# Reading the turned left-over rows back from DRAM: two plain DMAs of 64 rows ahead of the 128, in place of one with a repeated dimension

## The chip, the cores and the metric

The kernel runs on one core of one Trainium2 chip. The metric is the device time of one execution in microseconds (us). The time before is 1430.58 us, the median of 3 runs (1426.18 to 1431.6).

## The reference

Two parts follow one another. The first is a causal convolution over 7 taps whose weights are a softmax per token and head. The second is a gated feed-forward layer on the result. `x` is 4 x 4096 x 192, so there are 16384 tokens of 192 channels, in 8 heads of 24; the feed-forward width is 1536. All is float32.

```python
w = softmax(weight_gen, axis=-1)              # [B, S, 8 heads, 7 taps]
x_pad = concat([zeros(B, 6, 192), x], axis=1)
out = einsum('bshk,bskhg->bshg', w, windows_of_7(x_pad))
...
g = out @ w_gate                              # 192 -> 1536
y = (g * sigmoid(g)) * (out @ w_val) @ w_out  # 1536 -> 192
```

## The kernel before

The 16384 tokens lie as 128 partitions of 128 tokens. A block `g` takes 4 tokens (JG) of every partition, 512 tokens in all, and there are 32 blocks. For the matmuls a block is needed turned, channels on the partitions: 192 channels are one half of 128 and a left-over half of 64. Each float32 operand is split into a `hi` part in the fp32r format and the rest `lo`, and the products of the parts are summed in PSUM.

The feed-forward part goes in steps, 12 to a block (one for each 128 of the 1536 hidden channels), 384 in all. In a step TensorE makes the gate and the value sums (`up`, lines 500, 503 and 512). ScalarE takes the `silu` of one (`sg`, L520), VectorE multiplies (`h`, L534), ScalarE rounds it (`hi`, L535) and VectorE takes the rest (`lo`, L537). Two and three steps later TensorE multiplies by `w_out` (`dn`, L564, L573). There are four PSUM banks for `up`, two to a step; `sg` and `h` are what frees them.

The convolution of block `g` runs on VectorE beside the steps of block `g - 1`: products with a tap (`mul`, L234) and sums (`add`, L262), spread over the steps by hand (the function `spread` and the table `todo`). From block 2 on the result is turned in three moves (`turn_ops`). VectorE transposes within tiles of 32 x 32 (`blocks`, L341, into `cut`). Four DMAs on SP's queue write the tiles to a DRAM buffer `turned`, where they land in turned order (L352). Then SP reads them back into the tile `t32` of [128, 2, 512] (`places`): `t32[:, 0]` gets the 128 rows (L357). `t32[:, 1]` gets the 64 left-over rows twice, in partitions 0 to 63 and again in 64 to 127 (L358), since the left-over matmuls of the gate sums use the lower partitions and those of the value sums the upper ones. Reads wait until all four writes have landed.

Three steps after `blocks` and `places` comes the split of the turned block (`split_ops`), in the order `high(1)`, `low(1)` in one step and `high(0)`, `low(0)` in the next: ScalarE makes `xhi` (L378) and VectorE `xlo` (L385), the left-over half first. Engines work strictly in order, so what stands behind a waiting `xhi` on ScalarE, and behind a waiting `xlo` on VectorE, waits too. In the step of `high(1)` VectorE also has the first two products of the next block behind `xlo`.

This sets the order (`s0` is four steps before block `g - 1` begins):

```python
moves, halves = turn_ops(g)
at = s0 + NF - 3
spread(moves, at, at + 1)
spread(halves, at + 3, at + 5)
```

Of the kernel before, what the change touches and what calls it, by code (L numbers as in the profile page):

```python
# [18 lines left out]
def dynconv_glu_kernel(  # L19
# [23 lines left out]
    nc = tc.nc  # L43
    B, S, D = x.shape
# [3 lines left out]
    P = 128  # L48
    T = B * S // P
    PAD = K - 1  # L50
    DB = D - P
    JG = 4
    NC = JG * P
# [223 lines left out]
    LOW, HIGH = slice(0, DB), slice(DB, P)  # L277
# [54 lines left out]
    def turn_ops(g):  # L332

        whole = {}

        def blocks():
            cut = att.tile([P, JG, D], F32, tag="aside", name="cut", bufs=ASIDE)
            cut = whole["cut"] = cut.rearrange("p t d -> p (t d)").rearrange(
                "p (i t c) -> p i t c", i=NB, t=JG
            )  # L340
            nc.vector.transpose(  # L341
                cut, xatt[g][:, :, 0:D].rearrange("p t (i r) -> p i t r", i=NB)
            )

        def places():
            t32 = att.tile([P, JG, 2 * P], F32, tag="xatt", name="t32")
            t32 = whole["t32"] = t32.rearrange("p t d -> p (t d)").rearrange(
                "p (i n) -> p i n", i=2
            )
            there = away.tile([NB, Q, P // Q, P], F32, tag="turned", name="turned")  # L350
            for j in range(P // Q):
                nc.sync.dma_start(  # L352
                    out=there[:, :, j].rearrange("i r n -> r i n"),
                    in_=whole["cut"][j * Q : (j + 1) * Q].rearrange("r i t c -> r i (t c)"),
                )
            rows = there.rearrange("i r j n -> (i r) (j n)")
            nc.sync.dma_start(out=t32[:, 0], in_=rows[0:P])  # L357
            nc.sync.dma_start(  # L358
                out=t32[:, 1], in_=rows[P:D].unsqueeze(0).to_broadcast([2, DB, NC])
            )  # L360

        def part(n):
            def go():
                if n == 0:
                    t32 = whole["t32"]
                    whole["split"] = split_ops(g, (t32[:, 0], t32[:, 1]))
                whole["split"][n]()

            return go

        return [blocks, places], [part(n) for n in range(4)]

    def split_ops(g, ps):
        hi = [xts.tile([P, NC], F32R, tag=f"xhi{half}", name="xhi") for half in range(2)]

        def high(half):
            def go():
                nc.scalar.activation(out=hi[half], in_=ps[half], func=AF.Copy)  # L378

            return go  # L380

        def low(half):
            def go():
                lo = xts.tile([P, NC], F32R, tag=f"xlo{half}", name="xlo")
                nc.vector.tensor_tensor(  # L385
                    out=lo, in0=ps[half], in1=hi[half].bitcast(F32), op=ALU.subtract
                )
                xT[g, half] = hi[half], lo

            return go  # L390

        return [high(0), low(0), high(1), low(1)] if g < MOVED else [high(1), low(1), high(0), low(0)]
# [383 lines left out]
```

## Time and profile before

| | us |
|---|---|
| median of 3 runs | 1430.58 |
| the profiled execution | 1429.34 |
| its span, first to last instruction | 1427.6 |
| TensorE matmul busy (PE) | 1322.0 (93%) |
| VectorE busy (DVE) | 1026.0 (72%) |
| ScalarE busy (ACT) | 594.7 (42%) |
| GpSimd busy (POOL) | 62.4 (4%) |
| mean granted TensorE clock | 0.968 |

The profile is of one execution. Busy time of an engine is the time in which an instruction of it ran; matmuls are pipelined and their ends are modelled, so a busy TensorE isn't one at its peak. The list of waits gives the idle time of an engine just before an instruction and puts it down to what ended last. The windows give for a stretch of the span the busy time of each engine, the granted clock (1.00 is the level of 2.4 GHz, 0.50 that of 1.2) and the mean busy share of the 16 DMA engines.

### The profile page before, as it was taken

To read this page: it belongs to the slowest core of one execution; us is meant where nothing else is said; L and a number is where in the kernel's file an instruction comes from. 1 tells how busy PE (TensorE), PEld (TensorE's weight loads), DVE (VectorE), ACT (ScalarE), POOL (GpSimd) and SP (SyncE) were. 2 spreads that over 40 slices of the span, in tenths; PEclk is the share of its full clock that TensorE was granted. 3 is DMA by queue.
4 is the path that set the end of the run, shared out by engine and by line. 5 is a ranking of instruction groups with operands and counts; after the bars stand their busy time and mean duration, and the time that the engine had idled before them with its cause. 6 is when DMAs were issued, how large, how long until landed. Compare 5 with 4: busy or idle time off the path is not lost.

```text
span 1427.6 us, 31213 instructions
## 1 busy us (share of the span) xinstructions
PE 1322.0 (93%) x13184; PEld 1243.8 (87%) x13184; DVE 1026.0 (72%) x1413; ACT 594.7 (42%) x1049; POOL 62.4 (4%) x62
## 2 busy tenths in 40 slices
PE   5888999999999989999999999999999999999997
PEld 5677999888998978988898988988988898989997
DVE  6987677676777756787776687766677776677753
ACT  5444344433344434444443443433353433444443
POOL 4840000000000000000000000000000000000000
PEclk9799999999999999999999999999999999999999
DMA  6501211212211121211212111221211212110110
GB/s 173 172 12 46 77 36 26 65 27 77 58 44 49 35 65 38 72 34 41 77 27 77 38 33 56 54 66 38 74 26 27 68 35 77 38 27 24 38 38 12
DMA packets 63249, 74.88 MB, mean 52 GB/s; under 512 B 6024, under 2 KB 52616, under 8 KB 61316
## 3 DMA queue, kind: packets, MB, share of 16 engines
q1 hardware_dynamic: 63108, 72.88, 19.4%
q8 instruction: 103, 1.69, 0.5%
q14 instruction: 38, 0.31, 0.1%
HBM read 48.48 MB, written 24.38 MB: 51 GB/s over the span
## 4 chain that ended last, share of the span: by engine, by line
PE 47%; DMA 22%; DVE 19%; ACT 5%; SPq 4%; issue 2%; ACTq 0%; DVEq 0%
DMA t<-turned 17%; PE up L500 12%; PE up L512 11%; PE dn L564 10%; PE up L503 10%; DVE h L534 4%; DMA turned<-cut 4%; DVE prod L234 3%; SPq L352 3%; PE dn L573 3%; DVE xatt L234 2%; DVE cut L341 2%; ACT sg L520 2%; DVE xlo L385 2%; DVE lo L537 1%
## 5 line engine op out<-in xcount | busy, mean ns | idle before, releaser
L564 PE MATMUL dn<-wo,hi 64*128 64x384 f32 x2976 | 612.2, 351 | 1.4 <-ACT osb L589 1.1
L573 PE MATMUL dn<-wo,lo 64*128 64x192 f32 x2976 | 541.4, 252 | 0.3 <-DVE lo L537 0.3
L564 PEld LDWEIGHTS dn<-wo,hi 64*128 64x128 f32 x2976 | 507.0, 189 | 15.7 <-ACT osb L589 3.2
L573 PEld LDWEIGHTS dn<-wo,lo 64*128 64x128 f32 x2976 | 474.4, 191 | 3.5 <-DVE lo L537 0.5
L535 ACT ACTIVATE hi<-h 128x512 fp32r<-128x512 f32 x372 | 235.4, 633 | 386.2 <-DVE h L534 385.6
L534 DVE TENSOR_TENSOR h<-up,sg 128x512 f32<-128x512 f32 x372 | 256.1, 689 | 191.6 <-ACT sg L520 191.4
L520 ACT ACTIVATE sg<-up 128x512 f32<-128x512 f32 x384 | 228.0, 594 | 304.4 <-PE up L512 283.4
L500 PE MATMUL up<-xhi,wb_hi 64*128 64x512 f32 x768 | 250.0, 428 | 75.5 <-DVE h L534 55.5
L537 DVE TENSOR_TENSOR lo<-h,hi 128x512 fp32r<-128x512 f32 x372 | 254.9, 685 | 83.1 <-ACT hi L535 83.1
L512 PE MATMUL up<-xhi,wa_hi 64*128 64x512 f32 x768 | 233.0, 424 | 8.3 <-POOLq L282 8.2
L500 PE MATMUL up<-xlo,wb_hi 64*128 64x512 f32 x768 | 230.9, 404 | 1.5 <-DVE xlo L385 1.5
L500 PE MATMUL up<-xhi,wb_lo 64*128 64x512 f32 x768 | 227.3, 401 | 0.0
L503 PE MATMUL up<-xhi,wa_lo 64*128 64x512 f32 x768 | 227.1, 400 | 0.0
L503 PE MATMUL up<-xhi,wa_hi 64*128 64x512 f32 x768 | 226.5, 399 | 0.2 <-ACT xhi L378 0.2
L503 PE MATMUL up<-xlo,wa_hi 64*128 64x512 f32 x768 | 225.6, 397 | 0.0
L500 PEld LDWEIGHTS up<-xhi,wb_hi 64*128 64x128 f32 x768 | 136.6, 186 | 98.0 <-DVE h L534 70.0
L512 PE MATMUL up<-xhi,wa_lo 64*128 64x512 f32 x768 | 220.8, 395 | 0.0
L512 PE MATMUL up<-xlo,wa_hi 64*128 64x512 f32 x768 | 220.4, 393 | 0.0
L262 DVE TENSOR_TENSOR xatt<-xatt,prod 128x768 f32<-128x768 f32 x183 | 176.0, 962 | 0.0
L234 DVE TENSOR_TENSOR prod<-xt,wt 128x768 f32<-128x768 f32 x183 | 175.4, 958 | 0.2
L512 PEld LDWEIGHTS up<-xhi,wa_hi 64*128 64x128 f32 x768 | 137.0, 189 | 11.2 <-POOLq L282 11.2
L503 PEld LDWEIGHTS up<-xlo,wa_hi 64*128 64x128 f32 x768 | 139.1, 190 | 7.7 <-DVE xlo L385 0.5
(60 smaller groups left out, 1365.6 us busy)
## 6 DMA issues: line engine op xcount, KB each, us to landing
xt<-in_x_dram SPq DMA_DIRECT2D x14, 1344.0 KB, 11.6
t<-turned SPq DMA_DIRECT2D x60, 256.0 KB, 2.7
turned<-cut SPq DMA_DIRECT2D x120, 96.0 KB, 2.1
out_dram<-osb SPq DMA_DIRECT2D x116, 96.0 KB, 1.9
raw<-in_moe_w_out_dram SPq DMA_DIRECT2D x12, 192.0 KB, 2.8
wt<-in_weight_gen_dram SPq DMA_DIRECT2D x3, 672.0 KB, 9.6
raw<-in_moe_w_gate_dram SPq DMA_DIRECT2D x12, 128.0 KB, 2.1
raw<-in_moe_w_val_dram SPq DMA_DIRECT2D x12, 128.0 KB, 3.0
```

Of the source, the lines that this page charges most:

```text
L234: engine.tensor_tensor(out=into.rearrange("p t (h i) -> p t h i", h=H), in0=src, in1=w, op=ALU.mult)
L262: nc.vector.tensor_tensor(out=a, in0=a, in1=tmp.pop(k), op=ALU.add)
L352: nc.sync.dma_start(out=there[:, :, j].rearrange("i r n -> r i n"), in_=whole["cut"][j * Q : (j + 1) * Q].rearrange("r i t c -> r i (t c)"),)
L500: nc.tensor.matmul(ps, w[r, fs], m[r], start=(n == 0), stop=False)
L503: ins = nc.tensor.matmul(sums[i], w[r, i, fs], m[r], start=False, stop=False)
L512: ins = nc.tensor.matmul(sums[i], w[r, i, fs], m[r], start=False, stop=(n == len(full) - 1))
L520: nc.scalar.activation(out=sg, in_=sums[0], func=AF.Silu)
L534: nc.vector.tensor_tensor(out=h, in0=sums[1], in1=sg, op=ALU.mult)
L535: nc.scalar.activation(out=hi, in_=h, func=AF.Copy)
L537: nc.vector.tensor_tensor(out=lo, in0=h, in1=hi.bitcast(F32), op=ALU.subtract)
L564: nc.tensor.matmul(acc[t], hi[r, cs], wo[r, f].rearrange("p a d -> p (a d)"), start=opens, stop=False,)
L573: nc.tensor.matmul(acc[t][:, 0:D], lo[r, cs], wo[r, f, 0], start=False, stop=closes)
```

## The change

In `places` the read of the left-over rows with a repeated dimension goes. In its place two plain DMAs read the same 64 rows, one into partitions 0 to 63 (`LOW`) and one into 64 to 127 (`HIGH`) of `t32[:, 1]`. Both are issued ahead of the read of the 128 other rows, which came first before. Lines behind it move up by one, so L520 becomes L519 and so on.

```diff
             rows = there.rearrange("i r j n -> (i r) (j n)")
+            for r in (LOW, HIGH):
+                nc.sync.dma_start(out=t32[r, 1], in_=rows[P:D])
             nc.sync.dma_start(out=t32[:, 0], in_=rows[0:P])
-            nc.sync.dma_start(
-                out=t32[:, 1], in_=rows[P:D].unsqueeze(0).to_broadcast([2, DB, NC])
-            )
```

On SP's queue, in one of the blocks in which the load of `xt` follows, this is the order before, from the four writes to `turned` to the stores of a result (`t_16792` is the tile `t32` of that block; `DMAHW0` to `DMAHW7` are the semaphores that DMAs count in turn):

```order
L352 DMA turned<-cut 32x6x128 [waits DVE_49]
L352 DMA turned<-cut 32x6x128
L352 DMA turned<-cut 32x6x128 [waits DMAHW2_49]
L352 DMA turned<-cut 32x6x128 [waits DMAHW3_49]
L357 DMA t_16792<-turned 128x512 [waits DMAHW3_49,DMAHW2_49,DMAHW4_49,DMAHW1_49,DMAHW0_49]
L358 DMA t_16792<-turned 128x1x512 [waits DMAHW5_49]
L144 DMA xt<-in_x_dram 128x2688 [waits DMAHW6_49]
L605 DMA out_dram<-osb 32x4x192 [waits DMAHW7_49,DVE_49]
```

And this is the same place of the changed kernel:

```order
L352 DMA turned<-cut 32x6x128 [waits DVE_49]
L352 DMA turned<-cut 32x6x128 [waits DMAHW2_49]
L352 DMA turned<-cut 32x6x128 [waits DMAHW3_49]
L352 DMA turned<-cut 32x6x128 [waits DMAHW4_49]
L358 DMA t_16817<-turned 64x512 [waits DMAHW4_49,DMAHW3_49,DMAHW5_49,DMAHW2_49,DMAHW1_49]
L358 DMA t_16817<-turned 64x512 [waits DMAHW6_49]
L359 DMA t_16817<-turned 128x512 [waits DMAHW7_49]
L144 DMA xt<-in_x_dram 128x2688 [waits DMAHW0_49]
L604 DMA out_dram<-osb 32x4x192 [waits DVE_49]
```

Two reads became three, the 128 rows went from first to third, and the first read waits for the four writes as before.

On ScalarE the split of a block stands like this before, with the `silu` and the rounding of the steps around it:

```order
L520 ACTIVATE sg<-up 128x512 [waits PE_49,Activation_49]
L535 ACTIVATE hi<-h 128x512 [waits DVE_49]
L378 ACTIVATE xhi<-t_8734 128x512 [waits DMAHW3_49]
L520 ACTIVATE sg<-up 128x512 [waits PE_49,Activation_49]
L535 ACTIVATE hi<-h 128x512 [waits DVE_49]
L378 ACTIVATE xhi<-t_8734 128x512 [waits DMAHW2_49]
```

And in the changed kernel:

```order
L519 ACTIVATE sg<-up 128x512 [waits PE_49,Activation_49]
L534 ACTIVATE hi<-h 128x512 [waits DVE_49]
L377 ACTIVATE xhi<-t_8746 128x512 [waits DMAHW7_49,DMAHW6_49]
L519 ACTIVATE sg<-up 128x512 [waits PE_49,Activation_49]
L534 ACTIVATE hi<-h 128x512 [waits DVE_49]
L377 ACTIVATE xhi<-t_8746 128x512 [waits DMAHW0_49]
```

Nothing moved there; the first `xhi` waits for two reads where it waited for one.

## Rows read from the trace of the kernel before

**Rows 1.** The page, the chain that ended last, shares by line.

```profile
DMA t<-turned 17%; PE up L500 12%; PE up L512 11%; PE dn L564 10%; PE up L503 10%; DVE h L534 4%; DMA turned<-cut 4%; DVE prod L234 3%; SPq L352 3%; PE dn L573 3%; DVE xatt L234 2%; DVE cut L341 2%; ACT sg L520 2%; DVE xlo L385 2%; DVE lo L537 1%
```

**Rows 2.** Waits of the whole span: us in total, times, longest.

```profile
ACT xhi L378 <- DMA t<-turned: 107.2, 30, 7.1
```

**Rows 3.** Timeline of SP: start, length in us; one block, then the worst block.

```profile
462.37 1.80 SPq L352 DMA_DIRECT2D turned<-cut  x4
465.87 0.34 SPq L357 DMA_DIRECT2D t<-turned  x1
466.26 0.50 SPq L358 DMA_DIRECT2D t<-turned  x1
...
509.95 0.50 SPq L358 DMA_DIRECT2D t<-turned  x1
```

**Rows 4.** Timeline of ScalarE in that first block; brackets: idle before, and what ended it.

```profile
460.13 0.60 ACT L520 ACTIVATE sg<-up 128x512 f32<-128x512 f32 x1 [1.23 <-PE up L512]
...
469.77 0.60 ACT L520 ACTIVATE sg<-up 128x512 f32<-128x512 f32 x1 [1.22 <-PE up L512]
471.12 0.63 ACT L535 ACTIVATE hi<-h 128x512 fp32r<-128x512 f32 x1 [0.76 <-DVE h L534]
474.19 0.63 ACT L378 ACTIVATE xhi<-t 128x512 fp32r<-128x512 f32 x1 [2.43 <-DMA t<-turned]
```

**Rows 5.** Landings: of `t` where it could be matched; a 64-partition weight load.

```profile
DMA to landing us min/median/max: 2.6/2.7/2.8
...
raw<-in_moe_w_gate_dram SPq DMA_DIRECT2D x12, 64.0 KB, 2.4
```

**Rows 6.** Windows: stretch, length, busy us of each engine, clock, DMA share, GB/s.

```profile
470.00:473.50 3.50, 3.50 (x40) 3.48 (x38) 1.39 (x2) 1.00 (x2) 0.00 (x0) 1.00 0.13 51
```

**Rows 7.** Timelines of VectorE, then TensorE, behind that wait.

```profile
474.85 0.69 DVE L385 TENSOR_TENSOR xlo<-t,xhi 128x512 fp32r<-128x512 f32 x1 [2.37 <-ACT xhi L378]
476.33 0.95 DVE L234 TENSOR_TENSOR prod<-xt,wt 128x768 f32<-128x768 f32 x1
477.20 0.68 DVE L534 TENSOR_TENSOR h<-up,sg 128x512 f32<-128x512 f32 x1
...
477.94 0.49 PE L500 MATMUL up<-xhi,wb_hi 64*128 64x512 f32 x1 [1.50 <-DVE h L534]
```

**Rows 8.** Windows, five steps from the waiting one, per block; five of thirty, sum.

```profile
123.23:146.10 22.87, 19.20 (x172) 15.96 (x169) 17.11 (x26) 6.95 (x13) 0.00 (x0) 0.93 0.26 70
...
385.17:405.63 20.46, 18.37 (x173) 16.74 (x172) 14.96 (x21) 7.08 (x13) 0.00 (x0) 0.92 0.09 33
428.09:447.24 19.15, 17.05 (x174) 15.45 (x172) 14.44 (x21) 6.86 (x12) 0.00 (x0) 1.00 0.21 68
469.77:487.88 18.11, 16.61 (x173) 15.31 (x172) 13.72 (x20) 6.85 (x12) 0.00 (x0) 1.00 0.03 12
...
1368.18:1384.25 16.07, 16.07 (x174) 16.07 (x172) 8.02 (x12) 7.08 (x12) 0.00 (x0) 1.00 0.04 12
sum 601.73, PE 531.96 PEld 484.99 DVE 423.52 ACT 209.34 POOL 0.00; mean PE 17.73 PEld 16.17 DVE 14.12 ACT 6.98 POOL 0.00
```

**Rows 9.** Timeline of ScalarE, the waiting `xhi` of the other blocks named.

```profile
134.47 0.63 ACT L378 ACTIVATE xhi<-t 128x512 fp32r<-128x512 f32 x1 [3.62 <-DMA t<-turned]
...
390.60 0.63 ACT L378 ACTIVATE xhi<-t 128x512 fp32r<-128x512 f32 x1 [3.44 <-DMA t<-turned]
...
433.52 0.63 ACT L378 ACTIVATE xhi<-t 128x512 fp32r<-128x512 f32 x1 [3.45 <-DMA t<-turned]
...
519.48 0.63 ACT L378 ACTIVATE xhi<-t 128x512 fp32r<-128x512 f32 x1 [7.11 <-DMA t<-turned]
...
1372.53 0.63 ACT L378 ACTIVATE xhi<-t 128x512 fp32r<-128x512 f32 x1 [2.37 <-DMA t<-turned]
```

**Rows 10.** Windows around the idle TensorE of the block at 385.

```profile
393.00:394.00 1.00, 0.00 (x0) 0.00 (x0) 1.00 (x2) 0.00 (x0) 0.00 (x0) 1.00 0.00 0
395.00:397.00 2.00, 2.00 (x14) 1.62 (x12) 2.00 (x3) 0.96 (x2) 0.00 (x0) 0.50 0.00 0
```

## The prediction, made before the changed kernel had run

> **What bounds the kernel now.** I read the page's chain first, then the waits, then one block's pass in the timeline. The chain of work that ended last [rows 1] gives its largest single share to the transfer `t<-turned` (17% of the span; `t` is the tile `t32`, whose digits the views leave out). The list of waits says who pays: ScalarE's `xhi` stood idle for it 30 times, 107.2 us in all, 7.1 at the longest [rows 2]. There are 30 turned blocks (2 to 31), so this is one wait in each.
>
> The timeline of one block shows which of the two reads it is. SP issues the plain read (L357) at 465.87 and the repeated one (L358) at 466.26 [rows 3]. ScalarE runs a `silu` every 3.213 us (three steps from 460.13 to 469.77), finishes `hi` at 471.12 + 0.63 = 471.75, and then stands 2.43 us until `xhi` starts at 474.19 [rows 4]. That first `xhi` reads the left-over half `t32[:, 1]`, so it waits for the repeated read: 474.19 - 466.26 = 7.9 us from issue to landing. The plain read of the same size lands in 2.6 to 2.8 us [rows 5]. While only the repeated read is left, the mean busy share of the 16 DMA engines is 0.13 [rows 6], which is two engines out of sixteen. So it is slow because it lies on few engines, not because DMA is full.
>
> What the wait costs is not the wait itself, since ScalarE is not the last to finish; TensorE is. Behind `xhi` stand VectorE's `xlo` (474.85) and two products of 0.95 us (one stands in the rows), and only then `h` (477.20). TensorE's next `up` wants the PSUM bank that this `h` frees, and starts at 477.94 after 1.50 us idle [rows 7].
>
> To price it I cut, in each block, the five steps that begin with the waiting one. Undisturbed they are 5 x 3.213 = 16.07 us, which is exactly what the last block has, where the wait is 2.37 but no products of a next block stand behind it [rows 8, 9]. Two others at full clock have 18.11 with a wait of 2.43 and 19.15 with 3.45 [rows 4, 8, 9]. Both are 16.07 + wait - 0.38. So with products behind it the wait costs itself less 0.38 us, the slack TensorE has then. Another block has nearly the same wait (3.44) but 20.46, and its granted clock is 0.92 [rows 8, 9]. There TensorE idled through 393 to 394, and from 395 to 397 the granted clock was 0.50, the 1.2 GHz level instead of 2.4 [rows 10]. Such a drop costs 20.46 - 19.15 = 1.31 us. 16 of the 30 stretches show a clock under 1.00, none of them with a wait under 3.4.
>
> **The change, part by part.**
> - *The repeated read goes, two plain reads of 64 rows come, both before the 128 rows.* The bytes are the same (256 KB into `t32[:, 1]`). The first new read is issued where L357 is now, the second about 0.38 later, where L358 is now, since both wait for the same four landings. No row times a read of 64 rows by 2 KB. The nearest are the plain read of 128 rows by 2 KB (2.7) and the 64-partition loads of the weights (64 KB, 2.4) [rows 5]. The bounds are 2.4, and 5.0 if the second read moved only after the first (2 x 2.7 - 0.38). I take 2.7: each copy is half of the plain read, the two run together, and it is nearest that row. In the block shown, `t32[:, 1]` then lands at 466.26 + 2.7 = 469.0, and ScalarE wants it at 471.75, so the wait is gone with 2.8 us to spare.
> - *The worst block.* There L358 is issued at 509.95, and ScalarE is ready at 519.48 - 7.11 = 512.37 [rows 3, 9]. 2.42 us against 2.7 leaves a wait of 0.3, under the 0.38 that is hidden. Cost nothing.
> - *The 128 rows come third*, 0.7 to 0.8 us later than now. They land at about 465.87 + 0.8 + 2.7 = 469.4 and feed the second `xhi`, one whole step after the first. Nothing, and if the cover went, at most those 0.8 us a block.
> - *One more issue on SP* (0.34 us, 30 times) and one more semaphore in use. SP only issues DMAs. Behind the reads stand, in every second block, the load of `xt` and then the stores of a result that comes a good 20 us later. A wait for an older transfer could hold SP by a landing (2.7), and nothing on the way to the end listens. The `xt` load stays behind the reads. If it slows them as it may do now (waits of 3.45 beside 2.43), that is 1 us of the 2.8 to spare.
> - *ScalarE's first `xhi` now waits for two semaphores*, which is the later of the two landings, counted above.
>
> **The sum.** The thirty stretches last 601.73 us [rows 8]. 150 free steps last 150 x 3.213 = 482.0. The excess of 119.7 holds the waits (107.2, less 2.37 hidden in the last block, less 29 x 0.38 = 11.0, so 93.8), 16 blocks with a clock drop (some twice, about 23), and something of the first. That first stretch (it begins a step earlier) is 22.87 with a wait of 3.62 [rows 8, 9]. By the rule it would be 16.07 + 3.62 - 0.38 + 1.31 = 20.6, so 2.2 us there have another cause and stay. The change removes 119.7 - 2.2 = 117.5 us, 29 blocks down to 16.07. The profiled execution took 1429.34, 1.7 more than its span. **1429.3 - 117.5 = 1311.8, so 1312 us.** That execution lies 1.2 under the median of the runs (1430.58), which I leave in the range.
>
> Next in line is TensorE itself. In the last block's stretch it is busy for 16.07 of 16.07 us at clock 1.00 [rows 8], so below 3.213 a step this change has nothing to give.
>
> **Rivals.**
> 1. *The reads run one after the other*, and land 5.0 us after the second issue. Against 7.9 each wait shrinks by 2.9. Of the mean of 107.2 / 30 = 3.6 some 0.7 stays, 0.3 beyond the slack, and more in the late blocks: about 10 us, **1322**. For it: the copies share one queue. Against: the plain 128 rows, as many bytes as both copies, take 2.7. The Trainium skill (DMA: Bandwidth & Descriptors, Rules for kernel authors) speaks against the change here: it says not to bother with two transfers to disjoint partition halves, since they serialize on the same engines, and to use one transfer of 128 partitions. By that rule the pair would cost what this rival says at worst; the row of 7.9 shows that the single transfer here is not the good one the rule has in mind.
> 2. *The clock stays disturbed* though the idle time goes, because something else brings the drops. Then about 23 us remain: **1335**. Against: the stretches with waits under 3 us all show 1.00.
> 3. *Slower: 64 rows go onto one engine, and both copies onto the same one.* Today two engines carry 64 rows each in about 7.9 us. Then one engine carries 128, the second copy lands some 7 us later than the repeated read does, and 30 blocks lose 7 each: 210 us, **1640**. It decides at one point: whether the second copy lands later or earlier than 7.9 us after its issue. Against it: the 64-partition loads land in 2.4. The same page of the Trainium skill (Why a DMA increments its semaphore by 16 and not by 1) lets the number of engines follow from the slowest dimension, the largest number up to 16 that divides it. By that 64 rows would use all 16; no row here counts the engines of a 64-row read.
> 4. *Nothing changes*: the wait is for what the four writes to `turned` leave behind, and a plain read of these rows would be as late. **1429.** Against: the plain read is issued after the same four landings and lands in 2.7.
>
> **How the numbers follow.** The forecast has 0.82, rival 1 has 0.08, rival 2 has 0.05, a mix with half of the gain lost 0.01, rival 3 has 0.02 and rival 4 has 0.02. A difference of 0.5% (about 7 us) is what a measurement of this kernel can tell from none. Faster is 0.82 + 0.08 + 0.05 + 0.01 = 0.96, same 0.02, slower 0.02. The range goes down by the first block's 2.2 and by the spread of the runs (the lowest, 1426.18, is 4.4 below the median), to about 1304. Up it takes in rival 1 and 2 us of spread, to 1324. Rivals 2 to 4 and the mix are left out, with 0.1 and what the runs add.
>
> **What would show it.** Right: no wait of `xhi` on `t<-turned` of more than some 0.5 us; the five steps at 16.1 in all blocks but the first; no clock drop after the first blocks; TensorE's idle time before L500 down to the first stages. Wrong: `xhi` still waiting, with its landing at 5 (rival 1) or far beyond 8 (rival 3); steps of 3.2 with a clock of 0.92 (rival 2); or a new wait at `h`, if VectorE's two products alone are later than the 0.38 us allow.

## The result and the profile after

The changed kernel takes 1312.51 us (median of 4 runs, 1310.92 to 1312.98) against 1431.09 for the kernel before (4 runs). The ratio is 0.917, with a 95% interval of 0.914 to 0.920: faster by 8.3%. The forecast was 1312 in a range of 1304 to 1324.

The page of the changed kernel. Its span was 1427.6 before, and the chain that ended last began with 17% of `DMA t<-turned` [rows 1]:

```profile
span 1311.2 us, 31268 instructions
...
PE 1270.9 (97%) x13184; PEld 1242.9 (95%) x13184; DVE 1023.8 (78%) x1413; ACT 594.3 (45%) x1049; POOL 61.2 (5%) x62
...
DMA packets 64149, 74.88 MB, mean 57 GB/s; under 512 B 6924, under 2 KB 53516, under 8 KB 62216
...
PE 87%; DVE 6%; ACT 2%; DMA 2%; issue 1%; SPq 0%; POOL 0%; ACTq 0%; DVEq 0%; POOLq 0%
...
xt<-in_x_dram SPq DMA_DIRECT2D x14, 1344.0 KB, 6.8
...
t<-turned SPq DMA_DIRECT2D x60, 128.0 KB, 2.6
t<-turned SPq DMA_DIRECT2D x30, 256.0 KB, 3.0
...
wt<-in_weight_gen_dram SPq DMA_DIRECT2D x3, 672.0 KB, 4.4
```

The reads have left the chain, which is now TensorE for 87% of the span. The 64-row reads (128 KB each) land in 2.6 us in the median, the 128 rows in 3.0.

The view of the tile `t32` names the engine's idle time before its readers and who waited. Where the kernel before had 107.2 us of `xhi` [rows 2], the list is empty:

```profile
L377 ACT ACTIVATE xhi<-t x60: 612/616/634, 132.8 to 1257.1; 128x512 fp32r<-128x512 f32 x60
...
its engine sat idle before it (us, times) until:
who waited for it (us, times):
  PEld up L502: 1.3, 2
...
DMA to landing us min/median/max: 2.3/2.8/4.4
```

The thirty stretches of five steps [rows 8], cut in the same way from the profile after (stretch, length, busy us of PE, PEld, DVE, ACT and POOL, clock, DMA share, GB/s):

```profile
125.30:143.59 18.29, 17.52 (x174) 14.93 (x172) 16.09 (x24) 6.63 (x13) 0.00 (x0) 1.00 0.30 87
167.06:183.12 16.06, 16.06 (x174) 16.06 (x172) 14.73 (x21) 6.97 (x12) 0.00 (x0) 1.00 0.19 77
...
476.95:493.02 16.07, 16.07 (x175) 16.07 (x172) 14.00 (x20) 7.09 (x13) 0.00 (x0) 1.00 0.33 119
...
1252.26:1268.04 15.78, 15.78 (x171) 15.78 (x169) 8.12 (x12) 7.19 (x12) 0.00 (x0) 1.00 0.01 2
sum 483.88, PE 483.11 PEld 476.24 DVE 422.29 ACT 209.18 POOL 0.00; mean PE 16.10 PEld 15.87 DVE 14.08 ACT 6.97 POOL 0.00
```

Each is 16.06 or 16.07, but for the first (18.29) and the last (15.78), and each shows a clock of 1.00. The sum fell from 601.73 to 483.88, by 117.85 us, and the span by 116.4. The stretches between them (seven steps each) went from 683.0 to 682.6 in sum, and the start up to them took about 2 us more, for which no row here gives a reason. So the gain lies in these five steps a block.

In the timeline of SP and ScalarE, the block that had the longest wait (7.11, [rows 9]), then `hi` and `xhi` of the next block:

```profile
475.86 1.09 SPq L358 DMA_DIRECT2D t<-turned  x2
477.00 0.58 SPq L359 DMA_DIRECT2D t<-turned  x1
...
478.31 0.63 ACT L534 ACTIVATE hi<-h 128x512 fp32r<-128x512 f32 x1 [0.76 <-DVE h L533]
479.03 0.63 ACT L377 ACTIVATE xhi<-t 128x512 fp32r<-128x512 f32 x1
...
517.63 0.63 ACT L534 ACTIVATE hi<-h 128x512 fp32r<-128x512 f32 x1 [0.76 <-DVE h L533]
518.17 0.62 ACT L377 ACTIVATE xhi<-t 128x512 fp32r<-128x512 f32 x1
```

The second read is issued at about 476.4, and `xhi` begins at 479.03, 2.6 us later. It begins 0.72 us after `hi` began, where in the next block, and in all others, it is 0.54. So in the worst block `xhi` comes some 0.2 us late, which fits data that lands that late. The row shows no wait, and the five steps last 16.07 all the same.

### The profile page after: what moved, and what is told of

It is laid out like the page before. It is cut to its first block, busy times and chain, and to the rows that moved or that the text cites. A ratio compares the mean times of both kernels' runs of the same rounds, so it can differ in the third digit from the quotient of the medians.

```text
span 1311.2 us, 31268 instructions
## 1 busy us (share of the span) xinstructions
PE 1270.9 (97%) x13184; PEld 1242.9 (95%) x13184; DVE 1023.8 (78%) x1413; ACT 594.3 (45%) x1049; POOL 61.2 (5%) x62
## 2 busy tenths in 40 slices
DMA packets 64149, 74.88 MB, mean 57 GB/s; under 512 B 6924, under 2 KB 53516, under 8 KB 62216
## 4 chain that ended last, share of the span: by engine, by line
PE 87%; DVE 6%; ACT 2%; DMA 2%; issue 1%; SPq 0%; POOL 0%; ACTq 0%; DVEq 0%; POOLq 0%
PE up L511 23%; PE up L499 22%; PE dn L563 21%; PE up L502 18%; PE dn L572 2%; DVE h L533 1%; DMA xt<-in_x_dram 1%; DVE prod L234 1%; PE tr L300 1%; DVE lo L536 1%; PE dn L556 1%; ACT sg L519 1%; ACT L519 0%; ACT L186 0%; DMA raw<-in_moe_w_gate_dram 0%
## 5 line engine op out<-in xcount | busy, mean ns | idle before, releaser
L563 PE MATMUL dn<-wo,hi 64*128 64x384 f32 x2976 | 578.8, 344 | 0.8 <-ACT osb L588 0.4
L572 PE MATMUL dn<-wo,lo 64*128 64x192 f32 x2976 | 512.2, 249 | 0.3 <-DVE lo L536 0.3
L563 PEld LDWEIGHTS dn<-wo,hi 64*128 64x128 f32 x2976 | 477.4, 184 | 6.9 <-ACT osb L588 2.3
L572 PEld LDWEIGHTS dn<-wo,lo 64*128 64x128 f32 x2976 | 456.4, 186 | 1.8 <-DVE lo L536 0.5
L519 ACT ACTIVATE sg<-up 128x512 f32<-128x512 f32 x384 | 228.5, 595 | 302.4 <-PE up L511 295.4
L499 PE MATMUL up<-xhi,wb_hi 64*128 64x512 f32 x768 | 223.7, 418 | 8.1 <-DVE hi L528 5.9
L511 PE MATMUL up<-xhi,wa_hi 64*128 64x512 f32 x768 | 218.9, 419 | 10.5 <-POOLq L282 10.4
L499 PE MATMUL up<-xlo,wb_hi 64*128 64x512 f32 x768 | 211.5, 392 | 1.5 <-DVE xlo L384 1.5
L502 PE MATMUL up<-xhi,wa_hi 64*128 64x512 f32 x768 | 209.9, 391 | 0.2 <-ACT xhi L377 0.2
L502 PE MATMUL up<-xhi,wa_lo 64*128 64x512 f32 x768 | 209.6, 390 | 0.0
L502 PE MATMUL up<-xlo,wa_hi 64*128 64x512 f32 x768 | 208.8, 388 | 0.3 <-DVE xlo L384 0.3
L511 PE MATMUL up<-xhi,wa_lo 64*128 64x512 f32 x768 | 208.2, 391 | 0.0
L511 PE MATMUL up<-xlo,wa_hi 64*128 64x512 f32 x768 | 207.4, 389 | 0.0
L511 PEld LDWEIGHTS up<-xhi,wa_hi 64*128 64x128 f32 x768 | 127.2, 185 | 13.1 <-POOLq L282 13.1
L502 PEld LDWEIGHTS up<-xhi,wa_hi 64*128 64x128 f32 x768 | 128.4, 185 | 3.1 <-ACT xhi L377 0.7
```

Of the source, the lines that this page charges most:

```text
L499: nc.tensor.matmul(ps, w[r, fs], m[r], start=(n == 0), stop=False)
L502: ins = nc.tensor.matmul(sums[i], w[r, i, fs], m[r], start=False, stop=False)
L511: ins = nc.tensor.matmul(sums[i], w[r, i, fs], m[r], start=False, stop=(n == len(full) - 1))
L519: nc.scalar.activation(out=sg, in_=sums[0], func=AF.Silu)
L563: nc.tensor.matmul(acc[t], hi[r, cs], wo[r, f].rearrange("p a d -> p (a d)"), start=opens, stop=False,)
L572: nc.tensor.matmul(acc[t][:, 0:D], lo[r, cs], wo[r, f, 0], start=False, stop=closes)
```

## The experiments

The theory is the prediction's: the repeated read lies on two of the 16 DMA engines, so it lands late; ScalarE stands for it; five steps are lengthened by the wait less 0.38 us, and by a clock drop where there is one. The rivals are named in each.

### One part alone: the repeated read first

```diff
-            nc.sync.dma_start(out=t32[:, 0], in_=rows[0:P])
             nc.sync.dma_start(
                 out=t32[:, 1], in_=rows[P:D].unsqueeze(0).to_broadcast([2, DB, NC])
             )
+            nc.sync.dma_start(out=t32[:, 0], in_=rows[0:P])
```

> The kernel before, with the repeated read kept and only issued ahead of the 128 rows. Theory (the repeated read is slow because it lies on two DMA engines, and its landing is what costs): it lands only some 0.4 us earlier, since that is all that it is issued earlier. The 30 waits fall from 107 us to about 95, the time by 12 us and perhaps some clock drops: 1410 to 1420 us. Rival (the order of the reads is what brings the gain, the left-over rows were held up behind the 128 others): the wait goes, 1312 us.

Measured: 1418.79 us, ratio to the kernel before 0.992 (0.989 to 0.995). The view of `t32` in this kernel, the waits and the landing:

```profile
  DMA t<-turned: 97.9, 30
...
DMA to landing us min/median/max: 7.8/8.4/9.2
```

The waits fell from 107.2 to 97.9, which is 0.31 us in each of 30 blocks, where the read is issued 0.4 earlier. The order alone is worth 12 us of the 119 (7 to 16 by the interval), as the theory had it.

### The other part alone: two plain reads, behind the 128 rows

```diff
-            for r in (LOW, HIGH):
-                nc.sync.dma_start(out=t32[r, 1], in_=rows[P:D])
             nc.sync.dma_start(out=t32[:, 0], in_=rows[0:P])
+            for r in (LOW, HIGH):
+                nc.sync.dma_start(out=t32[r, 1], in_=rows[P:D])
```

> The changed kernel with its two reads of 64 rows issued behind the 128 rows, as the repeated read was. Theory (the spread over engines makes the gain, the order of the reads none): the pair is issued 0.4 to 0.9 us later and lands about 3.5 us after the 128 rows' issue, still some 2 us before ScalarE wants it; only the worst block may wait 1 us or so. 1312 to 1315 us. Rival (being first in the queue is part of the gain): waits of 1 us and more in many blocks, 1325 us or above.

Measured: 1313.92 us (1312.77 to 1316.82), ratio 0.920 (0.918 to 0.922). Of the changed kernel's gain all but about 1 us is there, and that 1 us is within the scatter of the runs. The wait comes back in five blocks, 4.3 us in all; in the worst one 1.47, and its five steps are 17.17 = 16.07 + 1.47 - 0.37:

```profile
481.94 0.63 ACT L377 ACTIVATE xhi<-t 128x512 fp32r<-128x512 f32 x1 [1.47 <-DMA t<-turned]
...
478.49:495.66 17.17, 16.67 (x174) 15.46 (x172) 13.74 (x20) 6.86 (x13) 0.00 (x0) 1.00 0.32 112
```

So the kind of read makes the gain. The order makes little once the reads are fast, but it is what keeps these five blocks free of waits.

### Plain reads on one, two and three engines

Each copy of 64 rows is cut in two so that the larger part has a count with few divisors. For one engine it is 61 and 3:

```diff
-            for r in (LOW, HIGH):
-                nc.sync.dma_start(out=t32[r, 1], in_=rows[P:D])
+            for r0 in (0, DB):
+                for k0, k1 in ((0, 61), (61, DB)):
+                    nc.sync.dma_start(out=t32[r0 + k0 : r0 + k1, 1], in_=rows[P + k0 : P + k1])
```

> The changed kernel with each copy of 64 rows read as 61 and 3. The Trainium skill (DMA: Bandwidth & Descriptors, Why a DMA increments its semaphore by 16 and not by 1) has the number of engines as the largest up to 16 that divides the rows; by that 61 rows go to one engine. Theory (the number of engines makes the landing): both copies lie on one engine, 122 rows where the repeated read had 64 on each of two. At (7.9 - 2) / 64 = 0.09 us a row they land about 13 us after the first issue. Waits of about 8 us in each of 30 blocks, 29 x 8 us and a clock drop or two in each: 1590 to 1640 us, slower than before. Rival (a plain read is fast and a repeated one slow, whatever the count of rows): 1312 to 1316 us.

The same with 62 in place of 61:

> The changed kernel with each copy of 64 rows read as 62 and 2, by the rule of the Trainium skill (DMA: Bandwidth & Descriptors, Why a DMA increments its semaphore by 16 and not by 1) on two engines each, the same two that the repeated read had. Theory (the number of engines is all): plain reads on two engines land like the repeated one, 7 to 9 us after the issue; some 100 us of waits and the clock drops come back: 1405 to 1435 us, the kernel before within 2%. Small packets: 2 + 2 + 2 + 2 engines in place of 2, so 6 x 30 = 180 more than before. Rival (a repeated dimension costs by itself, beyond the engines): clearly under 1400 us.

The same with 57:

> The changed kernel with each copy of 64 rows read as 57 and 7, by the same rule of the Trainium skill on three and on seven engines. Theory: three engines carry 38 rows each and a few of the seven; at 0.09 us a row the last lands about 5.7 us after the first issue, close to when ScalarE wants it. Some seventeen blocks wait little or not, twelve late ones 1 to 2 us: about 1327 us, 1314 to 1345. Rival (a plain read is fast whatever the count): 1312 to 1314 us, and no wait of xhi on the reads.

Measured: 1591.36 us with 61 (ratio 1.113, 1.109 to 1.117), 1441.41 with 62 (1.008, 1.004 to 1.013), 1345.50 with 57 (0.942, 0.938 to 0.946). The waits of `xhi` are 235.7, 117.1 and 37.1 us. For 61 rows, in a block with no load behind the reads, the issue, the wait, and the windows of the wait and of the five steps:

```profile
509.29 3.55 SPq L359 DMA_DIRECT2D t<-turned  x4
...
521.97 0.63 ACT L378 ACTIVATE xhi<-t 128x512 fp32r<-128x512 f32 x1 [6.73 <-DMA t<-turned]
...
516.00:520.00 4.00, 3.85 (x41) 3.61 (x37) 0.00 (x0) 0.00 (x0) 0.00 (x0) 1.00 0.07 25
...
513.25:538.02 24.77, 19.39 (x173) 17.72 (x172) 14.26 (x20) 7.07 (x12) 0.00 (x0) 0.86 0.06 20
```

A DMA share of 0.07 is one engine in 16, and the rows land 521.97 - 509.29 = 12.7 us after the first issue, where 13 was expected. For 62 rows the share in the wait is two engines, as it was for the repeated read (0.13, [rows 6]), and the wait of such a block is 2.21 where it was 2.43 [rows 4]:

```profile
475.00:478.00 3.00, 3.00 (x36) 3.00 (x34) 1.39 (x2) 1.23 (x2) 0.00 (x0) 1.00 0.13 49
...
479.37 0.63 ACT L378 ACTIVATE xhi<-t 128x512 fp32r<-128x512 f32 x1 [2.21 <-DMA t<-turned]
```

So a plain read on two engines is as slow as the repeated one, and the rival of a repeat that is slow by itself falls. The time came 6 us above the range given, and 12 above the kernel before. The four issues a block don't explain this: in the 13 blocks with no load behind the reads the waits add up to 38.1 us, against 39.6 before. In the 17 blocks with a load of `xt` or `wt` behind them it is 79.1 against 67.6, so the excess stands where the reads and a load are under way together. Why the repeated read suffers less from the load is open. For 57 rows the waits are short. The rule of 16.07 + wait - 0.38 holds to within 0.07 us in 23 of the 24 waiting blocks behind the first (waits under 0.38 cost nothing), and in one the stretch is 0.27 longer. Two of them (2.19 and 17.89, 3.19 and 18.88):

```profile
248.46 0.63 ACT L378 ACTIVATE xhi<-t 128x512 fp32r<-128x512 f32 x1 [2.19 <-DMA t<-turned]
490.13 0.63 ACT L378 ACTIVATE xhi<-t 128x512 fp32r<-128x512 f32 x1 [3.19 <-DMA t<-turned]
...
244.28:262.17 17.89, 16.66 (x174) 15.43 (x172) 13.73 (x20) 6.86 (x13) 0.00 (x0) 1.00 0.30 101
...
484.96:503.84 18.88, 16.79 (x174) 15.43 (x172) 13.73 (x20) 6.85 (x12) 0.00 (x0) 1.00 0.31 99
```

It was expected at about 1327 and came 0.5 us above the range, which ended at 1345. More blocks waited (25) than the twelve or so allowed for. What the expectation left out is the load: 26.6 of the 37.1 us of waits stand in the 17 blocks with a load behind the reads. There `xhi` starts up to 7.6 us after the first issue; in the blocks that wait without a load it is 5.8 to 6.2, near the 5.7 forecast.

The engines can also be counted from the page. Packets under 512 B before, with 61, with 62 and with 57 rows (DMA packets, MB, mean rate, counts by size):

```profile
DMA packets 63249, 74.88 MB, mean 52 GB/s; under 512 B 6024, under 2 KB 52616, under 8 KB 61316
```

```profile
DMA packets 63430, 74.89 MB, mean 47 GB/s; under 512 B 6204, under 2 KB 52796, under 8 KB 61496
```

```profile
DMA packets 63430, 74.89 MB, mean 52 GB/s; under 512 B 6204, under 2 KB 52796, under 8 KB 61496
```

```profile
DMA packets 63790, 74.89 MB, mean 56 GB/s; under 512 B 6564, under 2 KB 53156, under 8 KB 61856
```

Suppose that each engine that a DMA uses adds one small packet. Then the repeated read gives 2 a block. 61 and 3 rows twice give 1 + 3 + 1 + 3 = 8, 62 and 2 give 8, 57 and 7 give 20: 180, 180 and 540 more over 30 blocks, and that is what the counts show. They can't tell 61 rows from 62; the shares of 0.07 and 0.13 do. The changed kernel has 6924, 900 more, or 32 a block: 16 engines for each read of 64 rows. This is as the Trainium skill has it (DMA: Bandwidth & Descriptors, Why a DMA increments its semaphore by 16 and not by 1: the largest number up to 16 that divides the slowest dimension); the trace agrees at 61, 62, 57 and 64 rows and at the repeat of 2.

### The slow read kept, its reader a step later

```diff
-            spread(halves, at + 3, at + 5)
+            spread(halves, at + 4, at + 6)
```

This is the kernel before but for that line.

> The kernel before with its reads unchanged; the split of a turned block stands one step (3.2 us) later in the order. Theory (what costs is ScalarE standing at the wait, not the slow read itself): waits of up to 3.6 us vanish, twelve blocks with longer ones keep what is beyond that, some 11 us in all: about 1324 us, 1315 to 1340, with the repeated read still landing 7 to 9 us after its issue. Rival (the slow read costs by what it holds up elsewhere, the loads behind it in the queue and the clock): most of the loss stays, above 1380 us.

Measured: 1341.03 us, ratio 0.938 (0.935 to 0.941), 1 us above the range. Waits and windows of this kernel (TensorE's weight loads of L503 wait for the split in the first line):

```profile
PEld up L503 <- DVE xlo L385: 7.7, 20, 0.6
...
ACT xhi L378 <- DMA t<-turned: 11.3, 11, 2.9
...
123.49:147.81 24.32, 20.11 (x171) 16.42 (x169) 17.96 (x26) 6.96 (x13) 0.00 (x0) 0.86 0.23 66
...
487.42:509.20 21.78, 20.28 (x174) 17.84 (x172) 14.79 (x20) 7.07 (x12) 0.00 (x0) 0.84 0.27 88
...
571.64:588.10 16.46, 16.46 (x176) 16.02 (x174) 13.66 (x20) 6.92 (x12) 0.00 (x0) 1.00 0.23 75
```

The read is as slow as ever: in the worst block `xhi` starts 496.08 - 486.84 = 9.2 us after the issue, where it was 519.48 - 509.95 = 9.5 [rows 3, 9]:

```profile
486.84 0.50 SPq L358 DMA_DIRECT2D t<-turned  x1
...
496.08 0.63 ACT L378 ACTIVATE xhi<-t 128x512 fp32r<-128x512 f32 x1 [2.94 <-DMA t<-turned]
```

The waits that stay are the 11 us expected, and 90 of the 119 us are gone. So it is the standing ScalarE that costs, not the read. What the expectation left out is that a later split comes close to its own use: in twenty places TensorE's weight loads wait up to 0.6 us for `xlo`, and the first and the worst block (24.32 and 21.78, against 18.29 and 16.07 in the changed kernel) lose about 6 us each.

### One plain read of 128 rows

```diff
-            for r in (LOW, HIGH):
-                nc.sync.dma_start(out=t32[r, 1], in_=rows[P:D])
+            nc.sync.dma_start(out=t32[:, 1], in_=rows[DB:D])
```

> The changed kernel with one plain read of 128 rows in place of the two of 64. It reads the rows 64 to 191 of the turned block, so the lower half of the tile holds other rows than the reference needs; the bytes and the shape are those of a transfer without a repeat. This prices the rule of the Trainium skill (DMA: Bandwidth & Descriptors, Rules for kernel authors) that one transfer of 128 partitions is better than two on disjoint halves. Theory (both land well before ScalarE wants them, TensorE is the bound): within 0.3% of the changed kernel, 1309 to 1315 us; SP spends some 0.7 us less a block on issuing, and the read lands about as soon as the pair. Rival (two halves serialize and cost): more than 5 us faster than the changed kernel.

Measured: 1311.50 us (1310.66 to 1314.04), ratio 0.918 (0.916 to 0.920), the same as the changed kernel within the intervals. Its SP rows show the single read (L357) and then that of the 128 other rows (L358), and the small packets are 6444, 420 more than before, or 16 engines in place of 2:

```profile
514.96 0.34 SPq L357 DMA_DIRECT2D t<-turned  x1
515.34 0.43 SPq L358 DMA_DIRECT2D t<-turned  x1
...
DMA packets 63669, 74.88 MB, mean 57 GB/s; under 512 B 6444, under 2 KB 53036, under 8 KB 61736
```

So two halves cost nothing here that one transfer would save. The Trainium skill's advice (DMA: Bandwidth & Descriptors, Rules for kernel authors) against two transfers to disjoint halves shows only on SP, where the pair takes 1.09 us to issue and the single read 0.34, and the time shows nothing of it.

## Why the prediction was right

1. *The bound.* One wait of `xhi` in each of 30 blocks, with the reason in the number of engines: shown by the reads on one, two and three engines, whose time goes 1591, 1441, 1345.5, and 1313 on sixteen.
2. *The price of a wait*, itself less 0.38 us: read from the kernel before, and found again at waits of 1.47, 2.19 and 3.19 in two other kernels, and in 23 of 24 blocks of the second of them.
3. *The landing.* Taken as 2.7 us between 2.4 and 5.0; measured 2.6 in the median. The rival of serialized reads (1322) had 5.0, and the single read of 128 rows gains nothing on the pair.
4. *The worst block.* A wait of 0.3 under the slack was forecast. The row shows none, but `xhi` starts 0.2 late and the five steps are at 16.07, so this came out nearly as forecast. The pair behind the 128 rows has 1.47 in it.
5. *The 128 rows as third.* Forecast to land at no cost; they land in 3.0 us and the second `xhi` waits nowhere. The issuing on SP was mis-sized: one more issue of 0.34 was reckoned, but each read of 64 rows takes some 0.5. In the worst block the 128 rows went out 1.14 us after the first read (477.00 - 475.86) and not 0.7 to 0.8. That was covered too.
6. *The sum.* The stretches were to fall by 117.5 and fell by 117.85. The first was to keep 2.2 of its excess and has 18.29 - 16.07 = 2.22. What holds it is open; VectorE is busy for 16.09 of its 18.29 us. The last stretch is only shifted: it is 0.29 shorter, and the seven steps ahead of it are 0.27 longer. That the median of the runs came within 0.5 us of the forecast is luck in part: the runs before lie up to 9 us apart, the execution that the forecast started from lay 1.8 under their median, and the start took 2 us more.
7. *The clock.* All thirty stretches are at 1.00, so the drops came with the idle time of the wait, and the rival of a clock that stays disturbed (1335) falls.
8. *The slower rival* (both copies on one engine, 1640) did not come, but its mechanism is real: with 61 rows it gives 1591. Its price was too high: it put the landing 7 us later in each block, and with 122 rows on one engine the waits grew by (235.7 - 107.2) / 30 = 4.3.
9. *The bound behind it.* TensorE at 3.213 us a step, as in the last block before, is now every block's pace.

## What to carry to other kernels

When a transfer lands late although DMA is mostly idle, look at the mean share of the 16 engines while it alone is under way: 0.13 is two engines, and a leading repeat of two put it there. Price a wait from stretches of equal steps with different waits in the same trace; their differences give the part that is hidden and the price of a clock drop. The hidden part carried over to 0.1 us to four other kernels here, in all blocks at full clock but one (the first and the last block aside). The price of a drop (1.31) did so less well: with the repeated read first, the eleven stretches at 0.92 behind the first are 1.14 to 1.37 us over the rule. Where the transfer can't be made faster, its reader can be moved later, but only as far as the reader's own user allows.

## What was not expected

- The loads behind the repeated read had been slowed by it. `xt` of 1344 KB landed in 11.6 us before and lands in 6.8, `wt` of 672 KB in 9.6 before and 4.4 now. In the two other kernels that keep the repeated read `xt` takes 12.0 and 11.7, in the two others with plain reads on 16 engines 6.5 and 8.3. Before:

```profile
xt<-in_x_dram SPq DMA_DIRECT2D x14, 1344.0 KB, 11.6
...
wt<-in_weight_gen_dram SPq DMA_DIRECT2D x3, 672.0 KB, 9.6
```

- A read of 64 rows takes SP longer to issue (1.09 us for two) than one of 128 rows issued first (0.34, [rows 3]); the 128 rows issued third take 0.58 in the median, and up to 1.55.
- The clock drop doesn't follow the length of the wait alone. With the repeated read first, one stretch has a wait of 3.28 and a clock of 1.00, another 3.04 and 0.92. The last row is of the kernel before:

```profile
690.60 0.63 ACT L378 ACTIVATE xhi<-t 128x512 fp32r<-128x512 f32 x1 [3.28 <-DMA t<-turned]
944.92 0.63 ACT L378 ACTIVATE xhi<-t 128x512 fp32r<-128x512 f32 x1 [3.04 <-DMA t<-turned]
...
685.33:704.31 18.98, 16.90 (x174) 15.43 (x172) 14.44 (x21) 6.86 (x13) 0.00 (x0) 1.00 0.21 69
939.89:959.99 20.10, 18.02 (x174) 16.65 (x172) 14.87 (x21) 7.08 (x13) 0.00 (x0) 0.92 0.22 72
...
341.88:361.78 19.90, 17.05 (x174) 15.63 (x172) 13.69 (x20) 6.86 (x13) 0.00 (x0) 1.00 0.23 76
```

  In the kernel before no wait under 3.4 came with a drop, but this stretch has a wait of 4.21 and none (19.90 = 16.07 + 4.21 - 0.38). So 3.4 is no limit, and what decides whether a drop comes is open.
